# A gate multiplication moved from VectorE to GpSimd in seven blocks of a three-layer kernel

## The chip, the cores and the metric

The kernel runs on one core of one Trainium2 chip. Its time is the device time of one execution in microseconds (us), and the times given are medians of several executions. The engines are named as in the profile: PE is TensorE's matmul, PEld its weight load, DVE is VectorE, ACT is ScalarE, POOL is GpSimd, SP is SyncE, which here only issues DMAs (SPq is its queue). L1185 is line 1185 of the kernel's file.

## The reference

```
attention: q, k, v (4 batches, 8 heads, 576 rows, 64 wide), blockwise causal -> x [2304, 512]
layer one: h = x @ w_in [512, 2048];  x = (h - tanh(h)) @ w_out [2048, 512]
layer two: xn = x / rms(x) * rms_g
           g = xn @ w_gate [512, 1536];  val = xn @ w_val [512, 1536]
           out = (silu(g) * val) @ w_out2 [1536, 512]
```

Everything is float32 in and out. The change lies in layer two, in `silu(g) * val`.

## The kernel before

**Products.** A float32 operand is held as two parts, a high and a low one (`h`, `l`), and a product is three matmuls: high by high, high by low, low by high. Layer two works on pairs of token groups (384 tokens each, three passes) and on 12 blocks of 128 columns of `w_gate` and `w_val`. In each block the four half products of gate and value for the two halves of the tokens are made from seven products instead of eight, so sums stand between the products and the results. One block is one call of `fast`: seven products of six matmuls each, 42 matmuls of 128x384.

**A block's vector work.** The seven products leave PE in the order 1, 4, 5, 6, 0, 3, 2. DVE adds each to what came before (L1175, L1176, L1178, L1180, L1184), each with one operand in PSUM; ACT copies the first product (L1174) and makes the two gates (L1179, L1181). The second group's result is made by POOL (L1182: gate by value, both in SBUF). The first group's result is made by DVE at the block's end: L1184 adds `u` (SBUF) to the bank `lower` (PSUM), in place, and L1185 multiplies `lower` by the gate `gt` (SBUF) into the result tile in SBUF. The last product of a block is summed onto the bank `lower`, so its first matmul waits until L1178 has read that bank.

**Weights.** In pass one the weights of blocks three to nine are converted from their stored form while the blocks before them run. For each block two pieces are loaded (`st`), each goes through ACT (L149, L151) and DVE (L152, L153) into `fu`; three of the seven combinations are split into high and low at once (ACT L863, DVE L116 of 128x768), four are first combined on POOL (L854, L855, L857, L858, 128x256 each) and then split in three steps (ACT L871, DVE L116 of 128x512, 128x256 and 128x256). The finished tile `ws` is also stored for passes two and three (`keep`, L878, on SP's queue). Blocks ten and eleven load their finished tiles by DMA (L1145, the same queue, behind the stores of the blocks before). From block nine on, POOL forms sums over the results (`sums`, L1190).

**Order.** PE's instructions run in program order. From block ten on, DVE, ACT and POOL do so too; up to block nine, a planner orders each of these three engines' instructions by its own costs and due times when the kernel is built, with earlier program text first where several are ready. The seven blocks of the change all lie in the planned part.

Of the kernel before, what the change touches and what calls it, by code (L numbers as in the profile page):

```python
# [15 lines left out]
ALU = mybir.AluOpType  # L16
# [33 lines left out]
EARLY = 4  # L50
JH = J2 // 2
WHOLE = range(3, 10)
LAG = 2
SPLIT = 8
KEPT = 12
# [48 lines left out]
def build(ctx, tc, q, k, v, w_in, w_out, w_gate, w_val, w_out2, rms_g, ident_in, out):  # L104
    nc = tc.nc
    pin = tc.keep_in_program_order
    PE, ACT, DVE, POOL, SP = nc.tensor, nc.scalar, nc.vector, nc.gpsimd, nc.sync
# [542 lines left out]
    with tc.manual_schedule(engines={PE.engine}):  # L650
# [340 lines left out]
        for s in range(NSA):  # L991
            g, j = divmod(s, J1)
# [43 lines left out]
            gt = wk.tile([128, TG], F32, name="gt", tag="gt")  # L1036
# [13 lines left out]
            pend.append(s)  # L1050
            if len(pend) > LAG:
                n = pend.pop(0)
# [63 lines left out]
        def any_bank():  # L1116
            nonlocal nbank
            nbank += 1
            return chain_bank() if nbank % 8 in (6, 7, 0) else bank()

        def product(ps, wh, wl, xh, xl, first=True, last=True, more=False):
            nk = xh.shape[1]
            for kk in range(nk):
                c = slice(kk * 128, kk * 128 + 128)
                PE.matmul(ps, lhsT=wh[:, c], rhs=xh[:, kk], start=(first and kk == 0), stop=False, skip_group_check=more)  # L1125
                PE.matmul(ps, lhsT=wh[:, c], rhs=xl[:, kk], start=False, stop=False, skip_group_check=more)  # L1126
                PE.matmul(ps, lhsT=wl[:, c], rhs=xh[:, kk], start=False, stop=(last and kk == nk - 1),  # L1127
                          skip_group_check=more)
# [7 lines left out]
        def load_slot(q):  # L1136
# [4 lines left out]
            if j < J2:  # L1141
                if p == 0 and j in WHOLE:
                    direct[j].fill(w, 0)
# [6 lines left out]
        def temp(name, k, dt=F32):  # L1150
            return w2b.tile([128, k, TG], dt, name=name, tag=name, bufs=2)

        def result(n, j):
            if j not in G[n]:
                G[n][j] = w2g[j // 4].tile([128, TG], F32, name=f"g{n}_{j}")
            return G[n][j]

        def fast(s, j, x):

            w = slots.pop(s)  # L1160
            xa, xb, xc, xd = x

            def prod(n, xx, m, onto=None):
                ps = any_bank()[:, 0:TG] if onto is None else onto
                h, l = (y[:, 2 * m:2 * m + 2] for y in xx)
                product(ps, w[:, 0, n], w[:, 1, n], h, l, onto is None, True, onto is not None)
                return ps

            c11, va, vb = (temp(n, k) for n, k in (("c11", 1), ("va", 2), ("vb", 1)))
            c12, u = (va[:, n] for n in range(2))  # L1170
            c11, c22 = c11[:, 0], vb[:, 0]
            gt = wk.tile([128, TG], F32, name="gt", tag="gt")
            chain = prod(1, xa, 1)
            ACT.activation(out=c11, in_=chain, func=AF.Copy)  # L1174
            DVE.tensor_tensor(u, prod(4, xb, 1), c11, ALU.add)  # L1175
            DVE.tensor_tensor(c12, prod(5, xb, 0), u, ALU.add)  # L1176
            lower = prod(6, xc, 0)
            DVE.tensor_tensor(c22, lower, c12, ALU.add)  # L1178
            ACT.activation(out=gt, in_=prod(0, xa, 0, chain), func=AF.Silu)  # L1179
            DVE.tensor_tensor(c12, prod(3, xc, 1), c12, ALU.add)  # L1180
            ACT.activation(out=c12, in_=c12, func=AF.Silu)  # L1181
            POOL.tensor_tensor(out=result(1, j), in0=c12, in1=c22, op=ALU.mult)  # L1182
            prod(2, xd, 0, lower)
            DVE.tensor_tensor(lower, lower, u, ALU.add)  # L1184
            DVE.tensor_tensor(result(0, j), lower, gt, ALU.mult)  # L1185

        GS = [{}, {}]

# [144 lines left out]
        for p in range(NG // 2):  # L1333
            for j in range(J2):
                if p == 0 and j == WHOLE.stop:
                    ordered.enter_context(tc.manual_schedule(engines={DVE.engine, ACT.engine, POOL.engine}))
                if p == 0:
                    if j + 1 in WHOLE:
                        direct[j + 1].fill(slots[j + 1], 1)
                    if j + 1 < WHOLE.stop:  # L1340
                        direct[j + 1].keep()
                if p or j:
                    load_slot(p * NQ + j + 2)
                if p == 0:
                    if 5 <= j + 3 < WHOLE.stop:
                        direct[j + 3].piece(1)
                    if 5 <= j + 4 < WHOLE.stop:
                        direct[j + 4].load()
# [3 lines left out]
                if j == J2 - 1 and p == NG // 2 - 1:  # L1352
                    nbank = 0
                fast(p * NQ + j, j, x)
                for t in range(2):
                    n = j - t - (8 if p == 0 else 7)
# [35 lines left out]
```

## Time and profile before

| | |
|---|---|
| median of 3 runs | 1010.41 us (1010.19 to 1010.43) |
| the profiled execution | 1012.89 us |
| its span, first to last instruction | 1011.1 us |
| granted TensorE clock, mean | 0.998 of full speed |
| PE busy | 996.3 us, 99% of the span |
| DVE, ACT, POOL busy | 712.5, 661.3, 361.3 us |

The profile is of one execution, with the hardware profiler on; it is 2.48 us longer than the median of the runs without it. A row of a timeline gives the start of an instruction, its duration, engine, line, operation, output and inputs; in square brackets stands how long the engine was idle before it and what ended the idle time. Consecutive instructions of one engine overlap a little, so the cost of one on a busy engine is the distance from its start to the next one's start, not its duration.

### The profile page before, as it was taken

What the parts mean: (1) busy time and instruction counts of PE and PEld (TensorE: products, weight loads), DVE (VectorE), ACT (ScalarE), POOL (GpSimd) and SP (SyncE); (2) the same over time, 40 slices, a digit from 0 to 9 for tenths busy, and PEclk for the clock granted to TensorE, in tenths of its full rate; (3) what the DMA queues carried; (4) which work ended last, traced back from release to release, by engine and by line L of the source; (5) the groups of instructions that cost most, each with busy time, mean ns of one, the idle gap of its engine ahead of it and who ended that gap; (6) DMA issues with size and microseconds to landing.
All of it is one profiled execution on the core that took longest, in us unless ns stands there. A gap on an engine that the chain in (4) does not pass through costs nothing.

```text
span 1011.1 us, 18034 instructions
## 1 busy us (share of the span) xinstructions
PE 996.3 (99%) x5995; PEld 913.4 (90%) x5995; DVE 712.5 (70%) x1569; ACT 661.3 (65%) x1538; POOL 361.3 (36%) x538
## 2 busy tenths in 40 slices
PE   7999999999999999999999999999999999999998
PEld 5766888889988898889899889989999999999998
DVE  6878876876768777778767887976854458644565
ACT  6889987887888876788858775635732247412253
POOL 5522113332234252445334424575121470111710
PEclk9999999999999999999999999999999999999999
DMA  9799889874798699867969998987796757886664
GB/s 219 230 347 349 261 253 266 238 191 137 208 241 208 186 247 269 236 212 242 321 206 371 367 350 326 343 319 286 286 339 252 249 227 258 287 298 229 262 229 148
DMA packets 185420, 265.23 MB, mean 262 GB/s; under 512 B 109040, under 2 KB 150384, under 8 KB 178032
## 3 DMA queue, kind: packets, MB, share of 16 engines
q1 hardware_dynamic: 184240, 263.69, 80.7%
q8 instruction: 48, 0.79, 0.3%
q10 hardware_dynamic: 1088, 0.39, 0.1%
q14 instruction: 44, 0.36, 0.1%
HBM read 202.70 MB, written 61.34 MB: 261 GB/s over the span
## 4 chain that ended last, share of the span: by engine, by line
PE 79%; DVE 8%; ACT 5%; DMA 4%; issue 2%; SPq 1%; POOL 1%; DVEq 0%; ACTq 0%; POOLq 0%
PE t L775 5%; PE acc L808 5%; PE t L777 5%; PE t L776 5%; PE acc L810 5%; PE acc L809 5%; PE gv L1125 5%; PE gv L1127 5%; PE gv L1126 5%; PE t L581 4%; PE t L511 4%; PE ga L810 3%; PE ga L808 3%; PE ga L1127 3%; PE ga L809 3%; PE ga L1125 2%
## 5 line engine op out<-in xcount | busy, mean ns | idle before, releaser
L775 PE MATMUL t<-xh,w 128*128 128x384 f32 x384 | 138.8, 361 | 0.0
L777 PE MATMUL t<-xh,w 128*128 128x384 f32 x384 | 129.9, 338 | 0.4 <-DVE w L116 0.2
L776 PE MATMUL t<-xl,w 128*128 128x384 f32 x384 | 129.3, 337 | 0.0
L1125 PE MATMUL gv<-xh,ws 128*128 128x384 f32 x330 | 110.9, 336 | 0.5 <-DVE vb L1178 0.5
L1127 PE MATMUL gv<-xh,ws 128*128 128x384 f32 x330 | 110.9, 336 | 0.2 <-DVE ws L116 0.2
L1126 PE MATMUL gv<-xl,ws 128*128 128x384 f32 x330 | 110.7, 335 | 0.0
L808 PE MATMUL acc<-w,gh 128*128 128x512 f32 x264 | 109.1, 413 | 0.6 <-ACT gh L112 0.6
L810 PE MATMUL acc<-w,gl 128*128 128x512 f32 x264 | 104.4, 396 | 0.1
L809 PE MATMUL acc<-w,gh 128*128 128x512 f32 x264 | 103.9, 393 | 0.0
L1182 POOL TENSOR_TENSOR g<-va,vb 128x384 f32<-128x384 f32 x36 | 37.3, 1036 | 162.4 <-ACT va L1181 146.6
L552 ACT ACTIVATE pt<-pt,stat 128x64 f32<-128x64 f32 (+2 forms) x144 | 81.2, 564 | 17.6 <-DVE pt L550 12.3
L775 PEld LDWEIGHTS t<-xh,w 128*128 128x128 f32 x384 | 72.3, 188 | 7.3 <-issue 3.2
L776 PEld LDWEIGHTS t<-xl,w 128*128 128x128 f32 x384 | 72.5, 189 | 2.0 <-issue 0.5
L777 PEld LDWEIGHTS t<-xh,w 128*128 128x128 f32 x384 | 72.1, 188 | 1.0 <-DVE w L116 1.0
L116 DVE TENSOR_TENSOR gl<-gt,gh 128x384 fp32r<-128x384 f32 x88 | 58.6, 666 | 20.2 <-ACT gh L112 19.7
L116 DVE TENSOR_TENSOR pp<-t,pp 128x512 fp32r<-128x512 f32 (+3 forms) x112 | 55.3, 508 | 22.8 <-ACT pp L112 22.2
L581 PE MATMUL t<-ident,pt 128*128 128x128 f32 x400 | 65.0, 275 | 5.8 <-POOL pt L566 4.4
L581 PEld LDWEIGHTS t<-ident,pt 128*128 128x128 f32 x400 | 50.5, 141 | 18.4 <-POOL pt L566 5.4
L1043 DVE TENSOR_TENSOR gt<-t,gt 128x384 f32<-128x384 f32 x88 | 48.5, 551 | 25.0 <-ACT gt L1037 24.6
L112 ACT ACTIVATE pp<-t 128x512 fp32r<-128x512 f32 (+5 forms) x144 | 60.4, 437 | 8.0 <-PE t L581 6.7
L1125 PEld LDWEIGHTS gv<-xh,ws 128*128 128x128 f32 x330 | 62.0, 188 | 1.3 <-DVE vb L1178 1.1
L1127 PEld LDWEIGHTS gv<-xh,ws 128*128 128x128 f32 x330 | 61.9, 188 | 0.5 <-DVE ws L116 0.5
(210 smaller groups left out, 2947.4 us busy)
## 6 DMA issues: line engine op xcount, KB each, us to landing
ws<-w2d SPq DMA_DIRECT2D x26, 1792.0 KB, 7.5
ws<-wod SPq DMA_DIRECT2D x21, 1536.0 KB, 6.1
w<-w1d_i SPq DMA_DIRECT2D x60, 512.0 KB, 4.9
w<-w1d_o SPq DMA_DIRECT2D x52, 512.0 KB, 5.3
w2d<-ws SPq DMA_DIRECT2D x10, 1792.0 KB, 8.5
st<-in_moe_w_out SPq DMA_DIRECT2D x28, 512.0 KB, 5.8
st<-in_moe_w_in SPq DMA_DIRECT2D x16, 512.0 KB, 6.7
w1d_i<-w SPq DMA_DIRECT2D x16, 512.0 KB, 6.1
```

The costliest lines, as they stand in the source:

```text
L116: eng.tensor_tensor(out=o, in0=full, in1=hi.bitcast(F32), op=ALU.subtract)
L552: ACT.activation(out=pt[:, 0:keys], in_=pt[:, 0:keys], func=AF.Exp, scale=-1.0, bias=least, accum_out=st[:, 8 + ti:9 + ti])
L581: PE.transpose(t[:, (j - a) * 128:(j - a + 1) * 128], pt[:, j * 128:(j + 1) * 128], ident)
L775: PE.matmul(h, lhsT=wh[:, c], rhs=xh[:, kk], start=(kk == 0), stop=False)
L776: PE.matmul(h, lhsT=wh[:, c], rhs=xl[:, kk], start=False, stop=False)
L777: PE.matmul(h, lhsT=wl[:, c], rhs=xh[:, kk], start=False, stop=(kk == KD - 1))
L808: PE.matmul(acc, lhsT=gh[:, c], rhs=wh, start=first, stop=False, skip_group_check=more)
L809: PE.matmul(acc, lhsT=gh[:, c], rhs=wl, start=False, stop=False, skip_group_check=more)
L810: PE.matmul(acc, lhsT=gl[:, c], rhs=wh, start=False, stop=last, skip_group_check=more)
L1125: PE.matmul(ps, lhsT=wh[:, c], rhs=xh[:, kk], start=(first and kk == 0), stop=False, skip_group_check=more)
L1126: PE.matmul(ps, lhsT=wh[:, c], rhs=xl[:, kk], start=False, stop=False, skip_group_check=more)
L1127: PE.matmul(ps, lhsT=wl[:, c], rhs=xh[:, kk], start=False, stop=(last and kk == nk - 1), skip_group_check=more)
```

## The change

In blocks two to eight of pass one, the sum L1184 is written to the result tile in SBUF instead of back to PSUM, and the multiplication by the gate, which was L1185 on DVE, is done by POOL in place there. In blocks 0, 1 and 9 to 11 of pass one and in passes two and three nothing changes.

```
+SHARED = range(2, 9)
...
             prod(2, xd, 0, lower)
-            DVE.tensor_tensor(lower, lower, u, ALU.add)
-            DVE.tensor_tensor(result(0, j), lower, gt, ALU.mult)
+            if s in SHARED:
+                g = result(0, j)
+                DVE.tensor_tensor(g, lower, u, ALU.add)
+                POOL.tensor_tensor(out=g, in0=g, in1=gt, op=ALU.mult)
+            else:
+                DVE.tensor_tensor(lower, lower, u, ALU.add)
+                DVE.tensor_tensor(result(0, j), lower, gt, ALU.mult)
```

`s` counts the weight slots (19 in a pass: 12 blocks and 7 of the output product), so `s` from 2 to 8 are blocks two to eight of pass one alone.

## Rows read from the trace of the kernel before

**Rows 1.** The page's head and its busy times by engine.

```profile
span 1011.1 us, 18034 instructions
PE 996.3 (99%) x5995; PEld 913.4 (90%) x5995; DVE 712.5 (70%) x1569; ACT 661.3 (65%) x1538; POOL 361.3 (36%) x538
```

**Rows 2.** Timeline of DVE: last sum of blocks 0, 9 and 10.

```profile
607.78 0.57 DVE L1184 TENSOR_TENSOR gv<-gv,va 128x384 f32<-128x384 f32 x1 [0.77 <-PE gv L1127]
...
676.80 0.57 DVE L1184 TENSOR_TENSOR gv<-gv,va 128x384 f32<-128x384 f32 x1 [0.48 <-PE gv L1127]
...
684.12 0.57 DVE L1184 TENSOR_TENSOR ga<-ga,va 128x384 f32<-128x384 f32 x1 [0.48 <-PE ga L1127]
```

**Rows 3.** Waits of PE's weight loads, 620 to 676 us: total, times, longest.

```profile
PEld ga L1125 <- DVE vb L1178: 1.1, 2, 0.6
PEld gv L1125 <- DVE vb L1178: 0.7, 1, 0.7
PEld ga L1127 <- DVE ws L116: 0.6, 1, 0.6
PEld gv L1127 <- DVE ws L116: 0.5, 1, 0.5
PEld ga L1125 <- ACT ws L871: 0.5, 1, 0.5
```

**Rows 4.** Busy time by stretch, 622.4 to 668.5: PE, PEld, DVE, ACT, POOL, clock.

```profile
622.40:668.50 46.10, 45.08 (x254) 43.76 (x254) 43.20 (x77) 29.43 (x59) 22.65 (x25) 1.00 0.78 290
```

**Rows 5.** Timeline of DVE, blocks two, six, seven and nine.

```profile
622.42 0.57 DVE L1184 TENSOR_TENSOR ga<-ga,va 128x384 f32<-128x384 f32 x1 [0.48 <-PE ga L1127]
623.09 0.56 DVE L1185 TENSOR_TENSOR g<-ga,gt 128x384 f32<-128x384 f32 x1
623.57 1.35 DVE L116 TENSOR_TENSOR ws<-fu,ws 128x512 fp32r<-128x512 f32 x3
...
653.66 1.24 DVE L116 TENSOR_TENSOR ws<-fu,ws 128x256 fp32r<-128x256 f32 x1
...
661.99 1.23 DVE L152 TENSOR_SCALAR cv<-cv 128x512 f32<-128x512 f32 x1
...
670.73 0.95 DVE L116 TENSOR_TENSOR ws<-fu,ws 128x256 fp32r<-128x256 f32 x1 [0.20 <-ACT ws L871]
```

**Rows 6.** Timeline of POOL, blocks two, six, seven and eight.

```profile
622.63 1.02 POOL L1182 TENSOR_TENSOR g<-va,vb 128x384 f32<-128x384 f32 x1 [0.69 <-ACT va L1181]
...
653.44 1.18 POOL L1182 TENSOR_TENSOR g<-va,vb 128x384 f32<-128x384 f32 x1 [1.39 <-ACT va L1181]
...
661.93 1.01 POOL L1182 TENSOR_TENSOR g<-va,vb 128x384 f32<-128x384 f32 x1 [1.22 <-ACT va L1181]
...
669.14 1.10 POOL L858 TENSOR_TENSOR fu<-fu 128x256 f32<-128x256 f32 x1
670.20 1.19 POOL L1182 TENSOR_TENSOR g<-va,vb 128x384 f32<-128x384 f32 x1
```

**Rows 7.** DVE's conversion work by form, 622.4 to 668.5: busy, mean ns.

```profile
L152 DVE TENSOR_SCALAR cv<-cv 128x512 f32<-128x512 f32 x10 | 6.1, 607 | 0.0
...
L116 DVE TENSOR_TENSOR ws<-fu,ws 128x256 fp32r<-128x256 f32 x10 | 4.7, 495 | 0.0
L116 DVE TENSOR_TENSOR ws<-fu,ws 128x512 fp32r<-128x512 f32 x5 | 4.5, 903 | 0.0
```

**Rows 8.** The same work by line: shortest, median, longest ns, first and last start.

```profile
L152 DVE TENSOR_SCALAR cv<-cv x10: 409/421/1233, 624.8 to 662.0; 128x512 f32<-128x512 f32 x10
...
L116 DVE TENSOR_TENSOR ws<-fu,ws x20: 407/680/1240, 623.6 to 665.7; 128x256 fp32r<-128x256 f32 x10, 128x512 fp32r<-128x512 f32 x5, 128x768 fp32r<-128x768 f32 x5
```

**Rows 9.** SP's queue, the load for block ten, its time to landing, PE's block ten.

```profile
664.03 0.37 SPq L1145 DMA_DIRECT2D ws<-w2d  x1
...
ws<-w2d SPq DMA_DIRECT2D x1, 1792.0 KB, 12.1
...
676.60 0.34 PE L1125 MATMUL gv<-xh,ws 128*128 128x384 f32 x1
```

## The prediction

> **What bounds the kernel now.** I read the page first: PE is busy for 996.3 us of a span of 1011.1 [rows 1], so over the whole kernel PE sets the time, and work taken off DVE pays only where PE waits for DVE. So the next views are DVE's timeline and PE's waits around the seven blocks. A block's last sum starts when PE has delivered the block: blocks 9 and 10 end 7.32 us apart, undisturbed, and blocks 0 and 9 end 69.02 us apart [rows 2]. Nine undisturbed blocks would be 65.88, so PE loses 3.1 us in blocks one to nine. All of it is in six stops: three for DVE's L1178, which must have read the bank that the last product is summed onto, and three for weights of blocks eight and nine still being split (DVE L116, ACT L871) [rows 3]. The waits of the weight loads add up to 3.4, a little more than PE's own loss, since a load normally runs ahead of its matmul. These 3.1 us are the most that this change can give back by its own path, and 0.31% of the time.
>
> Why DVE is late is in the stretch from the end of block two to the end of block eight: DVE is busy for 43.20 of 46.10 us [rows 4], the rest being mostly short gaps between dependent instructions. Part of that busy time is not work. L152 takes 409 ns at its shortest and 607 in the mean, L116 of 128x256 407 and 495, L116 of 128x512 680 (the median of that line, which is this form) and 903 [rows 7, 8]. Times their counts (10, 10 and 5) the excess is 2.0 + 0.9 + 1.1 = 4.0 us. Two rows show where it comes from: an L116 of 0.41 took 1.24 us beside a POOL instruction of 653.44 to 654.62, and L152 took 1.23 us beside one of 661.93 to 662.94; both ended 0.28 us after POOL did [rows 5, 6]. DVE instructions without a PSUM operand are held up while POOL works; those with one are not: L1184 and L1185 of block two kept 0.57 and 0.56 us beside POOL's 622.63 [rows 5, 6].
>
> **The change part by part.**
>
> *Removed from DVE: seven L1185.* Each is 0.56 us long but costs the distance to the next start: 0.48 us, and 0.67 from L1184 to L1185, some 0.19 more than between independent neighbours, because it reads what L1184 wrote [rows 5]. In the seven blocks the cost lies between 0.48, where something stands between the two, and 0.67. I take 0.57: 7 x 0.57 = 4.0 us of DVE.
>
> *Changed: L1184's target.* PSUM becomes SBUF. L1184 took 0.57 us [rows 2] and 0.56 is what L1185 took from PSUM to SBUF [rows 5]: between nothing and 0.01 us each, taken as nothing. The bank `lower` comes free by one instruction earlier; no stop of PE is for a free bank after L1185 [rows 3], so this is worth nothing.
>
> *Added to POOL: seven multiplications of 128x384.* The same shape on the same engine is L1182, 1.01 to 1.19 us [rows 6]. In the stretch POOL is busy for 22.65 of 46.10 us [rows 4], so 7.1 us more fit, at nothing on POOL itself. What they cost is the hold on DVE. The lower end is 0 (it falls beside instructions with a PSUM operand, as in block two), the upper end is what the two rows show, 1.24 - 0.41 = 0.83 and 1.23 - 0.41 = 0.82 [rows 5, 8]. The existing L1182 cost DVE nothing in four of the blocks, 0.83 and 0.82 in two, and 0.95 - 0.41 = 0.54 behind block eight's, which ran from 670.20 to 671.39 [rows 5, 6, 8], 0.31 in the mean. But L1182 runs beside L1184 and L1185, which have a PSUM operand. The new instruction starts when L1184 has ended, where DVE comes out of its PSUM reads into conversion work: that work follows L1185 in five of the seven blocks. It also loses L1182 the cover of L1185: in block two L116 now waits at 623.57 [rows 5] and POOL is done at 623.65 [rows 6]; with L1185 gone it would be ready half a microsecond earlier and meet L1182. So I take a value above the mean of L1182 and below the two full collisions, nearer to the mean because two blocks continue with PSUM reads: 0.5 us each, 3.5 in all, with 0 and 5.8 as ends.
>
> The Trainium skill, "SBUF — State Buffer", Who interferes with whom, says that a VectorE instruction with two SBUF inputs, or in a two-port mode, and a GpSimd instruction that reads SBUF exclude each other for the whole instruction, whichever starts first. The two rows agree (both ended 0.28 us after POOL). By that rule in its strictest form each multiplication is a full collision, and the sum is that of the second rival below.
>
> *Order on POOL.* The new instruction stands behind L1182 and among the four combinations of the next weights, L854 to L858, in an order that the planner chooses. Behind them it delays nothing that PE waits for. Ahead of them it pushes the split of weights back by one POOL instruction, 1.0 us. In block eight this matters most: L858 ran at 669.14 [rows 6], and PE's last two stops are for the weights that it feeds [rows 3]. Cost: 0 to 1.0, taken as 0, since the combinations come earlier in the program and go first where both are ready. The next writer of `gt` is two blocks, 14.6 us, away, and covers the multiplication 14 times.
>
> *DMAs.* None is added. SP's queue is in order, and the load for block ten stands behind the store of block eight, which waits for DVE's last split of block eight. It went out at 664.03, took 12.1 us and so landed at 676.13; PE began block ten at 676.60 [rows 9]. Its slack is 0.47 us. If DVE finishes block eight's weights later, this load delays PE by what goes beyond 0.47. If PE gains only after 664, the load gives all but 0.47 of that back.
>
> *Sum.* DVE gets back 4.0 and loses 3.5: 0.5 us earlier at the end of block eight. PE's stops shorten by about that, since at each DVE is the late one or feeds it. 1012.89 for the profiled execution becomes 1012.4; the runs' median is 2.48 below the profiled time, so 1010.41 becomes **1009.9**. About 0.2% (2 us) is what a measurement of this kernel can tell from no change.
>
> **The rivals.**
>
> *The DVE time reaches PE (faster).* If a multiplication costs DVE 0.28 or less, near the 0.31 of L1182, DVE gains 4.0 - 2.0 = 2.0 or more, and PE's 3.1 us of stops mostly vanish: 1007.3 to 1008.4. For it: DVE is 94% busy in the stretch, and five of six stops name it. Against: the place behind L1184, and the load of block ten.
>
> *Collisions cost more than the multiplication did (slower).* The place is the instruction after L1184. At a price of 0.82, seven cost 5.7 against 4.0 freed: DVE is 1.7 us later at block eight, L1178 and the splits stop PE by so much more, and the load of block ten, issued later, no longer fits its 0.47 us. With one multiplication ahead of L858 it is 2.7. So 1012.1 to 1013.1. It decides from 0.57 each, where freed and lost are equal, and is measurable from 0.86, or from 0.72 with L858 delayed. For it: both rows of 1.2 us. Against: four of seven L1182 cost nothing. The Trainium skill, "Perfetto Trace Analysis", Optimizing Scalar/DVE Operations, warns that moving work between GpSimd and VectorE might not help, for the port they share; the 4.0 us of excess above are this kernel's measure of that.
>
> *The planner gives it another shape.* It reorders three engines by its own costs; removing an instruction from one can swap conversion and block work elsewhere. It may move the stops by about one stop, 0.5 us, either way: 1009.4 to 1010.9, inside the first case.
>
> **How the numbers follow.** Within 2 us of no change: 0.60, the forecast and the planner's case, 1008.4 to 1012.4. Faster by more: 0.21, bounded by 3.1 us. Slower by more: 0.19, bounded by nothing as hard. For 8 in 10 I go halfway into both: 1007.9 to 1012.5. So faster 0.21, same 0.60, slower 0.19.
>
> **What would show it.** Right: seven more POOL instructions of about 1.0 us beside the L1182, no L1185 from 622 to 670; DVE's time from block two to eight about 3 us shorter in instructions but with more excess in L152 and L116, about 7 instead of 4.0 us; L1184 of block nine at 676 to 677. Wrong on the fast side: the excess stays near 4 and the weight loads' 3.4 us of waits fall under 1.5. Wrong on the slow side: L116 or L152 of 1.2 us behind most L1184, L1178 later in each block, or a wait of PE for the load at block ten. The step most likely to fail is the 0.5 us of a collision, which no row shows in that place.

## The result, and the profile after

The changed kernel takes 1016.18 us (median of 6 runs, 1015.02 to 1018.64) against 1010.42 for the kernel before on the same chip: ratio 1.0052, 95% interval 1.0039 to 1.0066, so by the ratio 5.3 us slower (3.9 to 6.7). The ratios here and below are the recorded ones; they can differ a little from the quotient of the medians, and the ratio is what I use. The prediction was 1009.9 us, with 1007.9 to 1012.5 as its range and 0.19 for slower. It was wrong.

The profiled execution took 1015.02 us, 1.16 below the median of its runs, where that of before was 2.48 above its own: such an offset belongs to the execution and can't be carried from one kernel to the other. Its page has, against [rows 1], 7 instructions less on DVE, 7 more and 8.2 us more on POOL, and the same work on PE.

```profile
span 1013.0 us, 18036 instructions
...
PE 996.4 (98%) x5995; PEld 911.3 (90%) x5995; DVE 712.9 (70%) x1562; ACT 661.1 (65%) x1538; POOL 369.5 (36%) x545
```

All line numbers move, by one up to `fast` (the weights' lines) and by up to six behind it: DVE's conversion is now L153 and L154, its splits L117, the bank read that PE waits for L1179, the sum L1187 (L1190 in unchanged blocks), POOL's old multiplication L1183, the new one L1188, the store `keep` L879, the load L1146.

The two executions also differ ahead of the change. In the profiled execution of before, block 0's last sum starts at 607.78 [rows 2], in this one at 604.20, though nothing ahead of it differs in what is computed. The spans therefore show only 1.9 us of the loss. I compare from block 0's last sum on, by the starts of the last sums of blocks 9, 10 and 11, the milestones. From block 11's to the end of the span all executions below take 319.1 to 319.7 us. Timeline of DVE after:

```profile
604.20 0.57 DVE L1190 TENSOR_TENSOR gv<-gv,va 128x384 f32<-128x384 f32 x1 [0.77 <-PE gv L1128]
...
676.83 0.56 DVE L1190 TENSOR_TENSOR gv<-gv,va 128x384 f32<-128x384 f32 x1 [0.49 <-PE gv L1128]
685.11 0.57 DVE L1190 TENSOR_TENSOR ga<-ga,va 128x384 f32<-128x384 f32 x1 [0.49 <-PE ga L1128]
693.71 0.56 DVE L1190 TENSOR_TENSOR gv<-gv,va 128x384 f32<-128x384 f32 x1 [0.49 <-PE gv L1128]
```

Blocks 0 to 9 take 72.63 us instead of 69.02 [rows 2], +3.61. Block ten takes 8.28 instead of 7.32, +0.96. Block eleven takes 8.60 instead of 7.32, +1.28. Together +5.85, which agrees with the 5.3 of the runs. So the loss has two places: the seven blocks, and the two blocks behind them, in which nothing was changed.

The waits of PE's weight loads, from 617 to 688 us (total, times, longest), name the same two. DVE's splits L117 stop PE for 4.5 us instead of 1.1, L1179 for 1.9 instead of 1.8 [rows 3], and a DMA, which stopped nothing before, for 2.3:

```profile
PEld gv L1128 <- DVE ws L117: 2.8, 2, 1.4
PEld ga L1128 <- DVE ws L117: 1.7, 2, 1.1
PEld gv L1126 <- DVE vb L1179: 1.4, 2, 0.9
PEld ga L1126 <- DMA ws<-w2d: 1.3, 1, 1.3
PEld gv L1126 <- DMA ws<-w2d: 1.0, 1, 1.0
PEld ga L1126 <- DVE vb L1179: 0.5, 2, 0.3
PEld ga L1126 <- ACT ws L872: 0.5, 1, 0.5
```

DVE did not get less to do. The stretch below starts at block two's last sum, as [rows 4] does, and ends 1.06 us before block eight's (669.56), so that it holds the same conversion work and six of the seven changed blocks. In it DVE is busy for 45.52 of 49.67 us, against 43.20 of 46.10: 2.3 us more, with six multiplications less. POOL is busy 7.2 us more (same columns as [rows 4]):

```profile
618.83:668.50 49.67, 45.95 (x253) 43.60 (x252) 45.52 (x70) 29.50 (x59) 29.83 (x31) 1.00 0.74 262
```

The time is in the conversion work, by form in the same stretch (busy us, mean ns):

```profile
L154 DVE SCALAR_TENSOR_TENSOR fu<-cv,cu 128x512 int32<-128x512 int32 x10 | 9.8, 979 | 0.6
L153 DVE TENSOR_SCALAR cv<-cv 128x512 f32<-128x512 f32 x10 | 7.0, 705 | 0.0
L117 DVE TENSOR_TENSOR ws<-fu,ws 128x256 fp32r<-128x256 f32 x10 | 5.5, 576 | 0.0
L117 DVE TENSOR_TENSOR ws<-fu,ws 128x512 fp32r<-128x512 f32 x5 | 5.4, 1089 | 0.1
L117 DVE TENSOR_TENSOR ws<-fu,ws 128x768 fp32r<-128x768 f32 x5 | 5.2, 1044 | 0.0
```

Against [rows 7] L153 is 98 ns longer, the 256-wide split 81, the 512-wide 186. What is L154 now was L153 in before; there, in the stretch of [rows 7], it took 761 ns and the 768-wide split 949, so they are 218 and 95 longer.

```profile
L153 DVE SCALAR_TENSOR_TENSOR fu<-cv,cu 128x512 int32<-128x512 int32 x10 | 7.6, 761 | 0.2
L116 DVE TENSOR_TENSOR ws<-fu,ws 128x768 fp32r<-128x768 f32 x5 | 4.7, 949 | 0.0
```

Times 10, 10, 5, 10 and 5 that is 0.98 + 0.81 + 0.93 + 2.18 + 0.48 = 5.4 us, or 0.77 for each of the seven new POOL instructions (block eight's, outside the stretch, met no conversion work that took longer than before), where the prediction put the seven L1185 at 4.0 or 0.57 each. By these figures DVE's net is a loss of 1.4.

POOL's and DVE's timelines show one meeting, and a second thing:

```profile
644.81 1.44 DVE L117 TENSOR_TENSOR ws<-fu,ws 128x768 fp32r<-128x768 f32 x1
...
645.40 1.73 POOL L1188 TENSOR_TENSOR g<-g,gt 128x384 f32<-128x384 f32 x1
647.10 0.73 POOL L855 TENSOR_TENSOR fu<-fu 128x256 f32<-128x256 f32 x1
...
661.55 1.05 POOL L1188 TENSOR_TENSOR g<-g,gt 128x384 f32<-128x384 f32 x1 [1.17 <-ACT ws L872]
...
661.66 1.22 DVE L153 TENSOR_SCALAR cv<-cv 128x512 f32<-128x512 f32 x1
```

L153 at 661.66 ended 0.28 us after POOL's L1188 and took 1.22 us instead of some 0.41: the full collision of [rows 5, 6], now at the new place. That was block seven's. In block five's, POOL was the one held up: L1188 met a running L117 and took 1.73 us, and only then came L855, the first combination of the next weights. The planner had put the multiplication ahead of the combinations.

Last, SP's queue and PE behind the change:

```profile
665.11 0.37 SPq L1146 DMA_DIRECT2D ws<-w2d  x1
671.70 0.32 SPq L879 DMA_DIRECT2D w2d<-ws  x1
672.11 0.38 SPq L1146 DMA_DIRECT2D ws<-w2d  x1
...
677.48 0.44 PE L1126 MATMUL gv<-xh,ws 128*128 128x384 f32 x1 [0.69 <-DMA ws<-w2d]
...
686.08 0.44 PE L1126 MATMUL ga<-xh,ws 128*128 128x384 f32 x1 [1.02 <-DMA ws<-w2d]
```

The load for block ten went out at 665.11, 60.91 us after block 0's last sum; before it was 56.25 (664.03 - 607.78, [rows 9, 2]). That is 4.66 later for a PE that is 3.61 late, and the slack was 0.47; it landed after 12.3 us instead of 12.1. The load for block eleven now stands behind block nine's store (671.70); before it stood ahead of it, at 670.23. It took 13.9 us to land.

### The profile page after: what moved, and what is told of

Same layout as the page of the kernel before. It is cut to its first block, busy times and chain, and to the rows that moved or that the text cites. A ratio compares the mean times of both kernels' runs of the same rounds, so it can differ in the third digit from the quotient of the medians.

```text
span 1013.0 us, 18036 instructions
## 1 busy us (share of the span) xinstructions
PE 996.4 (98%) x5995; PEld 911.3 (90%) x5995; DVE 712.9 (70%) x1562; ACT 661.1 (65%) x1538; POOL 369.5 (36%) x545
## 4 chain that ended last, share of the span: by engine, by line
PE 77%; DVE 8%; ACT 6%; DMA 4%; issue 2%; SPq 1%; POOL 1%; DVEq 0%; ACTq 0%; POOLq 0%
PE t L776 5%; PE t L778 5%; PE acc L809 5%; PE t L777 5%; PE acc L811 5%; PE acc L810 5%; PE gv L1126 5%; PE gv L1128 5%; PE gv L1127 5%; PE t L582 4%; PE t L512 3%; PE ga L811 3%; PE ga L809 3%; PE ga L810 3%; PE ga L1126 2%; PE ga L1128 2%
## 5 line engine op out<-in xcount | busy, mean ns | idle before, releaser
L1183 POOL TENSOR_TENSOR g<-va,vb 128x384 f32<-128x384 f32 x36 | 37.4, 1039 | 158.1 <-ACT va L1182 158.1
L117 DVE TENSOR_TENSOR gl<-gt,gh 128x384 fp32r<-128x384 f32 x88 | 58.1, 661 | 20.2 <-ACT gh L113 19.7
L117 DVE TENSOR_TENSOR pp<-t,pp 128x512 fp32r<-128x512 f32 (+3 forms) x112 | 55.3, 507 | 23.2 <-ACT pp L113 22.8
```

Of the source, the lines that this page charges most:

```text
L117: eng.tensor_tensor(out=o, in0=full, in1=hi.bitcast(F32), op=ALU.subtract)
```

## The experiments

A change to one instruction lets the planner reorder four queues, SP's too, which the description of the kernel before doesn't say; so a plain variant mixes the edit with a new order. Most kernels below therefore write the order of DVE, ACT, POOL and SP for blocks 0 to 9 out by hand, as lists of each queue's instructions numbered in program order (ordering only, no semaphore). "In before's order" means that every instruction stands where it stood before.

```
+        def fix_order():
+            traced = nc.cur_bb.bb.instructions[mark:]
+            for engine, order in FIXED.items():
...
+                for m, n in zip(order, order[1:]):
+                    tc.add_manual_dep(mine[n], mine[m].name, mybir.DependencyInfo(
+                        mybir.DependencyClass.NoSync, mybir.DependencyReason.DATA), reason="order")
```

All times in one overview. "Profile" is the profiled execution: last sum of block 0 to that of block 9, block ten, block eleven, and the sum's difference to before (83.66 us). "Runs" is the ratio to before, with the kernel before run beside it each time (1010.42 to 1011.39 us).

| kernel | 0 to 9 | ten | eleven | diff. | median us | ratio (95%) |
|---|---|---|---|---|---|---|
| before | 69.02 | 7.32 | 7.32 | 0 | 1010.42 | 1 |
| after | 72.63 | 8.28 | 8.60 | +5.85 | 1016.18 | 1.0052 (1.0039, 1.0066) |
| n_nomult | 68.13 | 7.32 | 7.32 | -0.89 | 1010.67 | 0.9994 (0.9984, 1.0005) |
| d_double | 71.54 | 7.32 | 7.32 | +2.52 | 1013.13 | 1.0018 (1.0008, 1.0028) |
| x_order | 71.86 | 7.31 | 7.32 | +2.83 | 1013.42 | 1.0024 (1.0011, 1.0037) |
| x_order_late | 70.26 | 7.32 | 7.32 | +1.24 | 1014.27 | 1.0021 (1.0009, 1.0033) |
| m_write | 70.51 | 7.31 | 7.33 | +1.49 | 1012.64 | 1.0010 (0.9997, 1.0023) |
| y_neworder | 70.77 | 7.32 | 11.03 | +5.46 | 1015.35 | 1.0033 (1.0021, 1.0046) |
| y_spback | 70.78 | 7.32 | 7.32 | +1.76 | 1012.21 | 1.0010 (1.0001, 1.0019) |
| z_spback | 72.64 | 7.83 | 7.32 | +4.13 | 1015.62 | 1.0040 (1.0023, 1.0056) |
| s_st3 | 69.09 | 7.32 | 7.32 | +0.07 | 1015.68 | 1.0040 (1.0026, 1.0053) |
| n_st3 | 67.87 | 7.32 | 7.32 | -1.15 | 1016.13 | 1.0046 (1.0030, 1.0063) |

The two measures agree within about 1 us, except for y_neworder (one profiled execution with a longer stop) and for the last two, whose loss lies elsewhere. Two pairs of kernels have the same order and work on DVE, ACT and POOL (after and z_spback, y_neworder and y_spback): their blocks 0 to 9 agree within 0.01 us, so differences of a few tenths in that column are real. The runs resolve less: many of the intervals overlap.

### What is DVE's time worth? n_nomult and d_double

n_nomult leaves the seven multiplications out (the first group's results in blocks two to eight lack the gate), in before's order. It is the prediction's gain without its price.

```
             if s in SHARED:
                 g = result(0, j)
                 DVE.tensor_tensor(g, lower, u, ALU.add)
-                POOL.tensor_tensor(out=g, in0=g, in1=gt, op=ALU.mult)
```

> The multiplication is left out in the seven blocks (their first group's result lacks the gate), L1184 writes to SBUF, and every queue keeps the order of the kernel before. It prices the DVE time alone. If PE's 3.1 us of stops come from DVE being late, freeing 4.0 us of DVE with nothing put on POOL gives 1007.3 to 1008.5. If they come from somewhere else, 1010.4.

Measured: blocks 0 to 9 in 68.13 us, 0.89 less, and 0.9994 in the runs, whose interval holds 1. Of 4.0 us freed, PE sees 0.89. Timeline of DVE, then the weight loads that still wait:

```profile
605.51 0.57 DVE L1189 TENSOR_TENSOR gv<-gv,va 128x384 f32<-128x384 f32 x1 [0.74 <-PE gv L1128]
...
673.64 0.57 DVE L1189 TENSOR_TENSOR gv<-gv,va 128x384 f32<-128x384 f32 x1 [0.48 <-PE gv L1128]
```

```profile
PEld ga L1126 <- DVE vb L1179: 0.7, 1, 0.7
PEld ga L1128 <- DVE ws L117: 0.6, 1, 0.6
PEld ga L1126 <- ACT ws L872: 0.5, 1, 0.5
PEld gv L1128 <- DVE ws L117: 0.4, 1, 0.4
PEld gv L1126 <- DVE vb L1179: 0.2, 1, 0.2
```

Five of the six stops of [rows 3] are still there, three of them at their old length or longer: 0.7 for L1179 in block four (0.6 before), 0.5 for ACT and 0.6 for a split in block nine. From block two's last sum to block eight's DVE is busy 2.4 us less than in before (40.84 against [rows 4]), and its idle time grows from 2.9 to 4.3 us; PE gets 0.9.

```profile
620.15:665.31 45.16, 44.68 (x254) 43.78 (x253) 40.84 (x70) 29.43 (x59) 22.79 (x25) 1.00 0.79 293
```

A stop that names DVE is the end of a row of steps, load, ACT, DVE, POOL, ACT, DVE, and the freed time goes to waste in it in two ways. Ahead of the stop in block four DVE now waits 0.49 us for ACT, which waits 1.30 for the load of raw weights. At the last stop the split starts as soon as DVE is free, but beside POOL's last combination: it takes 0.87 us and ends 0.28 after POOL. In before the split waited for L1185 and then took 0.49; it ended 2.04 us after block eight's last sum in both kernels. Timelines of ACT, DVE and POOL in n_nomult, then of DVE in before:

```profile
630.42 0.67 ACT L150 ACTIVATE cv<-st 128x512 f32<-128x512 f32 x1 [1.30 <-DMA st<-in_moe_w_val]
631.12 0.74 DVE L153 TENSOR_SCALAR cv<-cv 128x512 f32<-128x512 f32 x1 [0.49 <-ACT cv L150]
...
665.96 1.10 POOL L859 TENSOR_TENSOR fu<-fu 128x256 f32<-128x256 f32 x1
666.48 0.87 DVE L117 TENSOR_TENSOR ws<-fu,ws 128x256 fp32r<-128x256 f32 x1
```

```profile
670.04 0.49 DVE L116 TENSOR_TENSOR ws<-fu,ws 128x256 fp32r<-128x256 f32 x1
```

For the comparison with x_order below, the same row of steps behind block five's last sum, at a place where PE doesn't wait (POOL, ACT, DVE):

```profile
644.40 1.39 POOL L1183 TENSOR_TENSOR g<-va,vb 128x384 f32<-128x384 f32 x1 [3.99 <-ACT va L1182]
...
647.49 0.63 ACT L872 ACTIVATE ws<-fu 128x512 fp32r<-128x512 f32 x1 [1.66 <-POOL fu L856]
...
648.16 1.15 DVE L117 TENSOR_TENSOR ws<-fu,ws 128x512 fp32r<-128x512 f32 x1
```

d_double is the mirror image: the multiplication twice on DVE, before's order.

```
             DVE.tensor_tensor(result(0, j), lower, gt, ALU.mult)
+            if 2 <= s < 9:
+                DVE.tensor_tensor(result(0, j), lower, gt, ALU.mult)
```

> The kernel before, every queue in its own order, with the multiplication by the gate in blocks two to eight issued twice on VectorE (the second writes the same product again; nothing is left out). VectorE has 7 x 0.56 = 3.9 us more work between the last sums of blocks two and eight, the mirror image of the run that leaves the multiplication out (there 4.0 us less work gave 0.89 us). Theory A (TensorE's stops come from a chain of single steps, load, conversion, combination, split, in which VectorE has room): from block 0's last sum to block 9's 69.5 to 70.5 us, 0.5 to 1.5 more than 69.02, and whole times within 0.2% of before. Theory B (VectorE is full there, and what is added to it arrives in full): 72.4 to 73.2 us, about 3.4 to 4.2 more, ratio 1.0035 to 1.004. B would also say that my prediction's step 'what VectorE gives up, TensorE gets' holds in one direction only.

Measured: 71.54 us, +2.52, ratio 1.0018: between the two theories. 3.9 us more cost 2.52 (0.65 for each us), 4.0 us less gave 0.89 (0.22 for each). Until block six the two kernels and before nearly keep step: n_nomult takes 47.17, d_double 47.40 and before 47.05 us from block 0's last sum to block six's, with four of the seven multiplications gone or doubled. The other three, 1.7 us, cost 2.2 behind that where they are doubled and give 1.0 where they are gone. So DVE has room up to block six and none behind it, and what DVE gets or gives up doesn't reach PE one for one in either direction.

### The price of POOL's multiplication: x_order, x_order_late, m_write

x_order is the change with all queues in before's order and L1188 right behind POOL's L1183, ahead of the combinations that follow there (in block four, ahead of two).

```
+            POOL.engine: [0, 1, 2, 3, 4, 5, 6, 7, 8, 9, 10, 11, 16, 17, 12, 13, 14, 15, 18, 19, 22, 23, 20, 21, 28, 29, 24,
...
```

> The change in full, but all four queues (DVE, ACT, POOL, SP) keep the order of the kernel before, with POOL's new multiplication right behind L1182 of the same block. Theory one (POOL's instruction holds DVE for more than the multiplication cost there): still slower than before, 1012 to 1014. Theory two (the planner's new order makes the weights late): 1009.5 to 1010.8, no different from before.

Measured: 71.86 us, ratio 1.0024. Against n_nomult, from which it differs only by the seven POOL instructions, +3.73 us or 0.53 each on PE. DVE's conversion grew by 3.3 us, 0.47 each (sum over the forms against n_nomult: L153 726 for 623 ns, L154 830 for 760, the 256-wide split 666 for 494, the 512-wide 955 for 984, the 768-wide 951 for 949). And the weights come later. The same place in the timeline, behind block five's last sum (POOL, ACT, DVE):

```profile
646.83 1.38 POOL L1183 TENSOR_TENSOR g<-va,vb 128x384 f32<-128x384 f32 x1 [2.93 <-ACT va L1182]
...
648.17 1.01 POOL L1188 TENSOR_TENSOR g<-g,gt 128x384 f32<-128x384 f32 x1
...
649.14 0.92 POOL L855 TENSOR_TENSOR fu<-fu 128x256 f32<-128x256 f32 x1
...
651.24 0.63 ACT L872 ACTIVATE ws<-fu 128x512 fp32r<-128x512 f32 x1 [2.99 <-POOL fu L856]
...
651.90 0.69 DVE L117 TENSOR_TENSOR ws<-fu,ws 128x512 fp32r<-128x512 f32 x1 [1.29 <-ACT ws L872]
```

From L1183 to the split it is 5.07 us here (651.90 - 646.83) and 3.76 in n_nomult (648.16 - 644.40): 1.31 later, and DVE stands idle for 1.29 of them, waiting for ACT, which waits for POOL. From block five's last sum to block six's it is 10.10 us instead of n_nomult's 9.26.

x_order_late puts L1188 behind the four combinations, wherever four stand there.

```
-            POOL.engine: [0, 1, 2, 3, 4, 5, 6, 7, 8, 9, 10, 11, 16, 17, 12, 13, 14, 15, 18, 19, 22, 23, 20, 21, 28, 29, 24,
+            POOL.engine: [0, 1, 2, 3, 4, 5, 6, 7, 8, 9, 10, 11, 16, 12, 13, 14, 15, 17, 18, 19, 22, 20, 21, 23, 28, 24, 25,
...
```

> As the change in the order of the kernel before, but POOL's multiplication stands behind the four combinations of the next weights, not ahead of them, so it delays no weights; it still reads SBUF while DVE converts. Blocks 0 to 9 took 69.0 us before, 71.9 with the multiplication ahead and 68.1 without any. If the loss is POOL holding DVE: 71 to 72. If it is the weights that POOL makes later: 68 to 69.5, and the whole kernel within 1 us of before.

Measured: 70.26 us, 1.60 less than x_order in the profiled execution; the runs (1.0021 against 1.0024) don't tell the two apart. It lies between the two forecasts. The wait of DVE for ACT is gone, but not the hold: the 256-wide splits, which now meet L1188, take 729 ns instead of 494 (DVE by form):

```profile
L117 DVE TENSOR_TENSOR ws<-fu,ws 128x256 fp32r<-128x256 f32 x10 | 7.1, 729 | 0.0
```

m_write puts two fills of the same tile in the place of each multiplication, so that POOL is as long in the way but reads nothing (the first group's results in seven blocks are zeros).

```
-                POOL.tensor_tensor(out=g, in0=g, in1=gt, op=ALU.mult)
+                POOL.memset(g, 0.0)
+                POOL.memset(g, 0.0)
```

> As the change in the order of the kernel before, with POOL's multiplication replaced by two fills of the same tile with zeros, which only write SBUF (the seven first-group results are zero). POOL's place and about its time are kept (a fill of 64x384 takes 0.41 us), but it reads nothing. If POOL's reading holds DVE, the means of L152, L153 and L116 fall back to those without the multiplication (0.62, 0.76, 0.56 and 0.93 us) and blocks 0 to 9 take 68 to 69.5 us. If the loss is the delay of the weights behind it on POOL, 71 to 72 as with the multiplication.

Measured: 70.51 us, +2.38 against n_nomult. DVE by form:

```profile
L154 DVE SCALAR_TENSOR_TENSOR fu<-cv,cu 128x512 int32<-128x512 int32 x10 | 7.8, 780 | 0.2
L153 DVE TENSOR_SCALAR cv<-cv 128x512 f32<-128x512 f32 x10 | 7.6, 757 | 0.0
L117 DVE TENSOR_TENSOR ws<-fu,ws 128x256 fp32r<-128x256 f32 x10 | 4.9, 502 | 0.2 <-ACT ws L872 0.2
L117 DVE TENSOR_TENSOR ws<-fu,ws 128x512 fp32r<-128x512 f32 x5 | 4.8, 953 | 1.6 <-ACT ws L872 1.4
```

The splits (502 and 953 ns) and L154 (780), with two inputs in SBUF, are close to n_nomult (494, 984 and 760); L153, with one, still takes 757 instead of 623. The late weights remain: the 512-wide split waits 1.6 us, as in x_order. So the two fills are not the order on POOL alone, and the run bounds rather than isolates. Of 3.73 us the place behind the combinations takes 1.60 away (x_order_late, in which the multiplication meets other work), and leaving out POOL's reads 1.35 (m_write, in which L153 is still held). That lateness and hold are both at work is shown; how much each is worth by itself is not. The Trainium skill, "SBUF — State Buffer", Who interferes with whom, makes this very difference: a VectorE instruction with two SBUF inputs collides with a GpSimd instruction that reads SBUF, not with one that only writes; one in a two-port mode collides with both. The means above agree, if L153 is of the two-port kind, which no run here shows by itself.

### The planner's order: y_neworder, y_spback, z_spback

y_neworder is the reverse of x_order: before's arithmetic, multiplication on DVE, with all four queues in the changed kernel's order.

```
+            SP.engine: [20, 21, 23, 24, 0, 1, 2, 3, 4, 5, 6, 7, 8, 9, 10, 11, 12, 13, 14, 15, 16, 17, 19, 18, 22],
...
```

> The kernel before, with the multiplication on DVE out of PSUM, but with the order of the four queues that the planner gave the changed kernel; L1185 stands right behind L1184. Theory one: near the kernel before, 1010 to 1011.5. Theory two: the loss is here too, 1013 to 1016.

Measured: 70.77, 7.32 and 11.03 us; ratio 1.0033. No instruction of before is changed, and three fifths of the change's loss is there in the runs (3.3 of 5.3 us). The planner's order of DVE, ACT and POOL costs 1.75 us by itself. The exchange on SP costs 3.71 in this execution: PE's weight load waits 2.17 us for the load of block eleven, and then the granted clock falls (windows, columns as in [rows 4]):

```profile
685.86:687.50 1.64, 1.64 (x9) 1.64 (x10) 0.08 (x1) 0.22 (x1) 1.56 (x2) 0.91 1.01 425
...
689.00:690.50 1.50, 1.50 (x6) 1.50 (x6) 0.56 (x1) 0.00 (x0) 0.00 (x0) 0.50 0.98 418
690.50:693.00 2.50, 2.50 (x16) 2.50 (x15) 1.11 (x2) 0.00 (x0) 0.00 (x0) 0.97 0.13 54
```

y_spback is the same with SP's last two DMAs exchanged back, z_spback the changed kernel with the same exchange.

```
-            SP.engine: [20, 21, 23, 24, 0, 1, 2, 3, 4, 5, 6, 7, 8, 9, 10, 11, 12, 13, 14, 15, 16, 17, 19, 18, 22],
+            SP.engine: [20, 21, 23, 24, 0, 1, 2, 3, 4, 5, 6, 7, 8, 9, 10, 11, 12, 13, 14, 15, 16, 17, 19, 22, 18],
```

> The kernel before (multiplication on VectorE) with VectorE's, ScalarE's and GpSimd's queues in the changed kernel's order, and SP's queue in the order of before. Nothing is left out. It takes the exchange of the last two DMAs out of the earlier run that had all four queues in the new order (70.77 us from block 0's last sum to block 9's, 7.32 to block 10's, 11.03 to block 11's). If the exchange alone makes the stop at block eleven: 70.3 to 71.2, 7.32, 7.32, so 1.3 to 2.2 more than before in all, ratio 1.001 to 1.0025. If the new order of the three engines makes the load late by itself, block eleven keeps more than 0.5 us of a stop.

> The changed kernel with its own order on DVE, ACT and POOL, and the last two DMAs of the stretch on SP's queue exchanged, as before: the load for block eleven goes ahead of the store of block nine's weights. If the wait of 1.3 us at block eleven comes from that exchange, it goes: about 1015.0 against 1016.2. If it comes from block nine being late, no change.

Measured: y_spback 70.78, 7.32, 7.32; z_spback 72.64, 7.83, 7.32. The stop at block eleven is gone in both: without the exchange there is none (the exchange with before's order of the three engines was not run). At block ten z_spback keeps half of the stop (+0.51 of +0.96), since the load's late issue remains. The other half is the load's time to landing, 12.3 us in the changed kernel and 11.9 here. In the kernels without the exchange that time ranges from 10.9 to 12.1, so whether the exchange made it, or one execution differs so from the next, isn't settled.

### Where do the old stops come from? s_st3 and n_st3

If freed DVE time is wasted because the raw weights arrive late, a third buffer for them (`st`) should help. s_st3 is before with it, n_st3 is n_nomult with it (and so without the seven multiplications).

```
-                    env["stg"] = sw0.enter_context(tc.tile_pool(name="st2", bufs=2, side="right"))
+                    env["stg"] = sw0.enter_context(tc.tile_pool(name="st2", bufs=3, side="right"))
```

> The kernel before, its order from block zero to nine fixed, with three stage buffers for the raw weights in place of two. If PE's stop at block four comes from a load that waits for a stage buffer (ACT waited 1.2 us for it), it goes: blocks 0 to 9 in 67.5 to 68.7 us against 69.0. If DVE's own work sets the stops, 69.0.

> Multiplication left out and three stage buffers. If two buffers are why freeing 4 us of DVE gave back 0.9 of PE's 3.1 us, the two together give 66 to 67 us for blocks 0 to 9 (65.9 is without any stop); if the chain through POOL and ACT is why, about 68.

Measured: blocks 0 to 9 in 69.09 (before 69.02) and 67.87 us (n_nomult 68.13): nothing, and 0.26, both where the second alternative was put. The whole kernels are 4.3 and 4.7 us slower, and that lies ahead of block 0, whose last sum starts at 611.06 and 610.72 instead of 604 to 608 in the other executions. There PE waits 4.2 us in s_st3 and 3.8 in n_st3 for a load of layer one's weights, which before doesn't, and the granted clock stands at 0.50, the 1.2 GHz level, for 6.8 us (595.7 to 602.5 in s_st3). In both, the first store of finished weights goes out ahead of the last two loads of layer one's (582.1 and 584.0 in s_st3), in before behind them; that this makes the wait was not tested. From block 0 on SP's order was fixed, so a load could not go out ahead of the DMAs that stood in front of it; a third buffer with another order on SP was not tried. What sets the stops of before that n_nomult leaves stays open between the loads' place on SP and the chain of steps behind them; for the one in block four and the last one, the rows of n_nomult above show where the freed time went.

## Why the prediction was wrong

**The loss, added up.** Each line is a difference of two profiled executions, from block 0's last sum to block eleven's; the last column is the same difference in the ratios, times 1010 and rounded:

| step | us | from | by the runs |
|---|---|---|---|
| DVE freed of seven L1185 | -0.89 | n_nomult - before | -0.6 |
| seven multiplications on POOL, order of before | +3.72 | x_order - n_nomult | +3.0 |
| the planner's new order of DVE, ACT and POOL | +1.30 | z_spback - x_order | +1.6 |
| SP's exchange | +1.72 | after - z_spback | +1.2 |
| sum | +5.85 | after - before | +5.3 |

The runs by themselves show the second step and the sum; the interval of the first includes zero, those of the last two overlap with their neighbours', and these three steps rest on the traces. The split depends on the way taken: by y_spback the order of the three engines costs 1.76 and the seven multiplications moved in that order 2.37 (z_spback - y_spback), where the table has 1.30 and 2.83 (-0.89 + 3.72). Of SP's 1.72, 0.45 are block ten's and not shown to be the exchange's.

**Freed: 4.0 us on DVE.** A little high: in n_nomult DVE's busy time falls by 3.0 us over the whole page (712.5 to 709.5), in part because some conversion work takes longer without L1185 (L153 623 for 607 ns, the 512-wide split 984 for 903). But the step that failed is the next one, "PE's stops shorten by about that, since at each DVE is the late one or feeds it". The 4.0 us gave PE 0.89. The stops end a chain over the load, ACT, DVE and POOL; in block four DVE came to wait for the load, and at the last stop for POOL. "DVE is busy for 43.20 of 46.10 us" said how full DVE was, not that PE waited for its fullness. The forecast had 4.0 - 3.5 = +0.5; with 0.89 in the place of 4.0 the same sum is a loss of 2.6. That x_order measured 2.83 is partly luck, since 1.60 of its loss goes away with the place on POOL, which the sum has at nothing. But the sign turns by this step alone: x_order_late, whose multiplication stands behind the combinations, still loses 1.24.

**Hold: 0.5 us for each multiplication.** Right in size with before's order, 0.47 each on DVE, though 0.5 was a choice between 0 and 0.83 and not read from a row. In the changed kernel, with its own order, it was 0.77 each, near the 0.82 of the slower rival. The forecast's excess in L152 and L116 was 7 instead of 4.0, a rise of 3; those two lines rose by 0.98 + 0.81 + 0.93 + 0.48 = 3.2. L154, which the prediction had left out of its count, rose by another 2.2.

**Order on POOL: taken as 0.** Failed. The argument was that the combinations stand earlier in the program and go first where both are ready. In the changed kernel the new multiplication ran ahead of three of the four combinations in block three and of all four in blocks four (with L1183 between) and five; only in the other blocks did none follow at once. In before's order the place is worth 1.60 us over seven blocks by the profiled executions (x_order - x_order_late), 0.23 each.

**The load for block ten: slack 0.47.** Right as a mechanism, and it was paid: issued 4.66 us later for a PE 3.61 later, it came 0.58 beyond the slack, and block ten lost 0.96. Not seen was the load behind it. The prediction looked at what stands ahead of block ten's load and not at whether the order of SP's queue itself could change.

**The planner: 0.5 us either way, inside "same".** Failed by size. Three engines' order cost 1.30 us (1.75 in y_spback, with the multiplication on DVE), SP's exchange another 1.72. That is half of the loss by the table, and neither is a property of the multiplication.

**L1184's target and the bank: nothing.** No run contradicts it; L1187 takes 0.54 to 0.57 us as L1184 did.

**The rivals.** The slower one had all its three parts right (collisions above 0.57 each, the combinations later, the load of block ten) and was still too small, 1012.1 to 1013.1, since it too counted the freed 4.0 us in full and took the planner's part for zero. The faster one is refuted in its ground: even at a price of nothing the gain is 0.89 us in the profile and can't be told from none in the runs. For the same reason no other place for these seven multiplications promises a measurable gain while the orders stay as they were; an order made for the freed DVE was not tried.

## What to carry to other kernels

An engine that is 94% busy and that the waits name is not yet a bound: leave the work out altogether first. Here that costs one kernel and shows that the most to be won in this order is 0.9 us. Where a planner orders the queues, one moved instruction can change all of them, as it did here, the DMA queue too; hold the order fixed to price the instruction, and apply the new order to the old arithmetic to price the order. Between VectorE and GpSimd, price the place as well as the length: whom the instruction meets, and what stands behind it on its queue.

## What the runs showed of the hardware

- **A stop of PE can cost twice.** In y_neworder PE's weight load waited 2.17 us for a DMA, with the granted clock at 1.00 (the 2.4 GHz level) before it. Some 1.3 us after PE had resumed the grant fell to 0.50, the 1.2 GHz level, until about 690.6, and matmuls that followed each other at 0.17 us did so at 0.32. From 687.2 to 690.6 that is 3.4 us at half speed, 1.7 lost: with the 1.85 us for which PE itself was idle it makes 3.55 of the 3.71 of block eleven. The stop at the same place in the changed kernel, 1.34 us for the weight load and 1.02 for PE, left the clock at 1.00.
- **Fills on GpSimd hold some VectorE work.** L153 (one SBUF input) took 757 ns in the mean beside two fills per block and 623 without; at 662.71 in m_write it took 1.60 us and ended 0.28 after the first fill. Instructions with two SBUF inputs kept their time: the 256-wide split at 664.23, beside the second fill throughout, took 0.41.
- **The hold goes both ways.** L1188 took 1.01 us in x_order where it started beside no DVE work or work with a PSUM operand, and 1.73 in the changed kernel where it met a running L117 of 128x768.
